# Polysketch attention, then an ELU feed-forward: group 0's division moved behind x, other rounding of the weights, z behind the keys' outer products

## The chip, the cores and the metric

The kernel runs on one core of a Trainium2 chip. The metric is the device time of one execution in microseconds (us). The weights and the sketches S1, S2 arrive as 64-bit floats, which the kernel reads as two 32-bit words each; q, k and v are float32.

## The reference

Four batches, four heads, 1088 positions, head size 32. Queries and keys are turned into features by two 8 x 32 sketches, and linear attention is formed with them; then comes a feed-forward layer with ELU.

```python
r = 8
def phi(x):                       # 64 features: outer product of two sketches
    a = np.einsum('rd,bhsd->bhsr', S1, x)
    b = np.einsum('rd,bhsd->bhsr', S2, x)
    return np.einsum('bhsi,bhsj->bhsij', a, b).reshape(*x.shape[:-1], r * r)
q_p, k_p = (phi(q), phi(k))
kv = np.einsum('bhsf,bhsd->bhfd', k_p, v)
z = np.sum(k_p, axis=2)
num = np.einsum('bhsf,bhfd->bhsd', q_p, kv)
den = np.einsum('bhsf,bhf->bhs', q_p, z)[..., None] + 1e-06
attn = num / den
...
h = x @ w_in                      # x: 4352 x 128, w_in: 128 x 2048
g = np.where(h > 0.0, h, np.exp(np.minimum(h, 0.0)) - 1.0)
out = g @ w_out                   # 2048 x 128
```

## The kernel before

**Groups and pairs.** The 4352 rows of x are cut into groups `g` of 512 columns; x of a group is held transposed (`xg[g]`, 128 features by 512 rows). The hidden layer of 2048 is cut into eight pairs `cp` of two 128-blocks `c`. `mm1(g, cp)` makes `h` in PSUM (four "h" banks, two for a step), `elu_a` is two ScalarE instructions (relu of -h, exp), `elu_d` one VectorE instruction that makes `gg`, and `mm2(g, cp)` sums the output. Every matmul is cut into column strips of 32 (`quarters`) and each shows as two records.

**Order.** The kernel gives every engine its instructions in the order in which the program names them (`manual_schedule`). Nothing is reordered: an instruction that waits holds all that is named after it on its engine. First come the setup and group 0 by hand, then group 1's queries mixed with the first steps, and then a loop over `steps`: (0,0), (0,1), (1,0), (1,1), (0,2), (1,2), (0,3), ... as (g, cp). Steps 0 and 1 are written by hand; the loop begins with step 2. In step n it does mm1, the work listed under `at(n)`, ELU of block 0, the work under `mid(n)`, ELU of block 1, the work under `late(n)`, and then mm2 (for group 1 `mm2_blocks`) of step n-2.

**Queries of group 0.** `q1_first` gives the two sketches of the queries (`abq`), `q1z_first` the sketch times z (`zqp`). `q2_den` multiplies and sums them to `den`, takes the reciprocal and multiplies one sketch by it (`an`); `q2_out` makes the outer products `qp`; `q4_early` turns them (`qtp`, copied to `qpT`); `q5_early` multiplies by the key sums `kvS` and copies to `xg[0]`. Group 1 goes the same way through `q1_second`, `q2(1, 2)`, `q4_early(1)`, `q5_early(1)`.

**Keys of batch 0.** `KF(0)` makes the sketches, `KO_pool` (POOL) the outer products of tiles 0 to 3, `KO_first` (VectorE) those of tiles 4, 5 and 6, 7 and 8, `KA(0)` the key sums in PSUM (`kv`), `KS_first` turns them into `kvS`. `Z` and `Z_out` give z's sketch in `SW`.

**Weights.** TensorE multiplies in float32, and the 64-bit weights are rounded in the kernel. They are loaded raw (`raw`, words lo and hi) on the SP queue, and a chunk `i` of `order` is rounded into `W`: chunks 0 and 1 are w_in of pairs 0 and 1, chunks 2 and 3 their w_out, 4 and 5 w_in and w_out of pair 2, chunks 6 to 10 all of pairs 3 to 7 (512 columns). The steps are `round_a` (VectorE), `round_b` (ScalarE), `round_s`, `round_m`, `round_d`, `round_e` (VectorE; for chunk 7 `round_e` on POOL). RA, RB, RC name them in groups.

Of the kernel before, what the change touches and what calls it, by code (L numbers as in the profile page):

```python
# [15 lines left out]
MUL, ADD, SUB, MAX = ALU.mult, ALU.add, ALU.subtract, ALU.max  # L16
AND, OR, SHL = ALU.bitwise_and, ALU.bitwise_or, ALU.logical_shift_left
EXP = mybir.ActivationFunctionType.Exp
RELU = mybir.ActivationFunctionType.Relu
AX = mybir.AxisListType.X  # L20
# [7 lines left out]
def kernel(  # L28
# [21 lines left out]
    nc = tc.nc  # L50
# [43 lines left out]
    nc.vector.memset(ebias[:], -float(896 << 23))  # L94
    tiny = const.tile([P, 1], F32, name="tiny")
    nc.gpsimd.memset(tiny[:], 2.0 ** -20)

# [17 lines left out]
    def round_s(raw, dst):  # L115
        d = dst.bitcast(U32)
        nc.vector.scalar_tensor_tensor(d, words(raw)[1], 0x80000000, d, op0=AND, op1=OR)

    def round_m(raw, dst):
        hi = words(raw)[1]  # L120
        nc.vector.tensor_scalar(hi, hi, 0x000FFFFF, 0x00100000, op0=AND, op1=OR)

    def round_c(raw, dst):
# [6 lines left out]

    def round_e(raw, dst, pool=False):
        mant = words(raw)[0].bitcast(F32)
        if pool:
            nc.gpsimd.tensor_mul(mant, mant, _ap(tiny[:], [[0, dst.shape[1]]]))  # L134
            nc.gpsimd.tensor_mul(dst, mant, dst)
        else:
            nc.vector.scalar_tensor_tensor(dst, mant, 2.0 ** -20, dst, op0=MUL, op1=MUL)

# [40 lines left out]
    def round_w(f, i, *a):  # L179
        if wide:  # L180
            cp, w_in, w_out = order[i]
            c = slice(0 if w_in else 2 * P, 4 * P if w_out else 2 * P)
            f(raw_w[cp][:, c], W[:, cp, c], *a)

    def RA(i):
        round_w(round_a, i)

    def RB(i):
        round_w(round_b, i)


    def RC_2():
        if wide:
            for f in (round_s, round_m, round_d):
                f(raw_2[:, :, :2 * P], W[:, :2, :2 * P])

    def RS(i):
        round_w(round_s, i)

    def RM(i):  # L200
        round_w(round_m, i)

    def RD(i):
        round_w(round_d, i)

    def RE(i):
        round_w(round_e, i)

    def RC(i, pool=False):
        round_w(round_c, i)  # L210
        round_w(round_d, i)
        round_w(round_e, i, pool)

# [207 lines left out]
    def z_tile(b, ps, i):  # L421
# [4 lines left out]
                         skip_group_check=True, tile_position=(0, c))  # L426

    def KA(b, halves=(0, 1)):
        if 0 in halves:
            kv_ps[b] = psum.tile([P, 512], F32, name="kv", **(dict(tag="aux") if b else dict(tag="o1", bufs=1)))  # L430
        kv = kv_ps[b]
        kp = {half: feats.pop((b, half)) for half in halves}
        for i in range(0 if 0 in halves else 5, KT if 1 in halves else 5):
            for h in range(H):
                nc.tensor.matmul(kv[32 * h:32 * h + 32, :R * R], vt[b][:, (h * KT + i) * D:(h * KT + i + 1) * D],  # L435
                                 kp[i // 5][:, i % 5, h].rearrange("p i j -> p (i j)"),
                                 start=(i == 0), stop=(i == KT - 1), skip_group_check=True, tile_position=(0, 32 * h))
            if b:
                z_tile(b, kv, i)

# [37 lines left out]

    def KS_first():
        kd = work.tile([P, 2, R * R], F32, name="kd", tag="kd", bufs=1)  # L480
        nc.scalar.copy(kd[:], _ap(kv_ps[0][:, :R * R], [[0, 2], [1, R * R]]))
        nc.tensor.transpose(kv_ps[0][:, 128:256], kd[:].rearrange("p w f -> p (w f)"), ident[:])
        nc.scalar.copy(kvS[:].rearrange("p h d -> p (h d)"), kv_ps[0][:, 128:256])
# [37 lines left out]
    def q1_second():  # L521
        p = psum.tile([P, 512], F32, name="abwp", tag="h", bufs=4)
        for i in range(4):
            for u in range(2):
                b, t = half_tile(1, 2 * i + u)
                nc.tensor.matmul(p[64 * u:64 * u + 64, i * 96:i * 96 + 96], qT[b][:, t, :],
                                 SW[:].rearrange("p h x r -> p (h x r)"), skip_group_check=True,
                                 tile_position=(0, 64 * u))
        abw[1] = work.tile([P, H * 4, 3 * R], F32, name="abw1", tag="abq1", bufs=1)
        nc.scalar.copy(abw[1][:].rearrange("p (h t) y -> p h t y", h=H),  # L530
                       p[:, :384].rearrange("p (t h y) -> p h t y", t=4, h=H))


# [47 lines left out]
    def q2_den(g, zq=None, between=None):  # L581
# [11 lines left out]
        nc.vector.tensor_reduce(den[:, :m], pw[:, :m], axis=AX, op=ADD)  # L593
        nc.vector.reciprocal(den[:, :m], den[:, :m])
        an = work.tile([P, 8 * H, R], F32, name="an", tag="an")
        nc.vector.tensor_mul(an[:, :m], x[:, :, R:2 * R], _ap(den[:, :m], [[1, m], [0, R]]))
        ans[g] = an

    def q2_out(g, parts=1, between=None):
        m = H * qn[g]  # L600
        x, an = abw.pop(g), ans.pop(g)
        qp[g] = work.tile([P, 4 * H, R, R], F32, name="qp", tag="qp", bufs=2)
        for i in range(parts):
            if i and between:
                between()
            h = slice(i * m // parts, (i + 1) * m // parts)
            a_ = an[:, h]
            b_ = x[:, h, :R]
            nc.vector.tensor_mul(qp[g][:, h], _ap(a_, list(a_.ap[1:]) + [[0, R]]),  # L609
                                 _ap(b_, [b_.ap[1], [0, R], b_.ap[2]]))  # L610

    def q4_early(g):

        qpT[g] = work.tile([P, H, 2, P], F32, name="qpT", tag="qpT", bufs=2)
        for hh in range(2):
            p = psum.tile([P, 512], F32, name="qtp", tag="aux")
            for h2 in range(2):
                for m in range(2):
                    o = (h2 * 2 + m) * P
                    r = (2 * hh + h2) * 4 + 2 * m  # L620
                    nc.tensor.transpose(p[:, o:o + P], qp[g][:, r:r + 2].rearrange("p t i j -> p (t i j)"), ident[:])  # L621
            nc.scalar.copy(qpT[g][:, 2 * hh:2 * hh + 2], p[:].rearrange("p (h m s) -> p h m s", h=2, m=2))

    def q5_early(g):
        xp = [psum.tile([P, 512], F32, name="xps", tag="aux") for _ in range(2)]
        for h in range(H):
            for w in range(2):
                nc.tensor.matmul(xp[w][D * h:D * h + D, :256], kvS[64 * w:64 * w + 64, h, :],  # L628
                                 qpT[g][64 * w:64 * w + 64, h].rearrange("p m s -> p (m s)"),
                                 skip_group_check=True, tile_position=(64 * w, D * h))  # L630
        xg[g] = work.tile([P, 512], F32, name="xg", tag="xg", bufs=3)
        to = xg[g][:].rearrange("p (m w s) -> p w m s", w=2, s=P)
        for w in range(2):
            nc.scalar.copy(to[:, w], xp[w][:, :256].rearrange("p (m s) -> p m s", s=P))  # L634

# [211 lines left out]
    def mm1_first():  # L847
        hs[0, 0] = [psum.tile([P, 512], F32, name="h", tag="h", bufs=4) for c in range(2)]
        for w in range(2):
            for c in range(2):  # L850
                cols = [x[:].rearrange("p (m w s) -> p w m s", w=2, s=P)[:, w] for x in (hs[0, 0][c], xg[0])]
# [23 lines left out]

    def mm2(g, cp, first, last):
        n = qn[g] * P
        if first:
            ops[g] = psum.tile([P, 512], F32, name="o", tag=f"o{g % 2}", bufs=1)
        gg = gs.pop((g, cp))  # L880
        for c in range(2):
            quarters(ops[g][:, :n], W[:, cp, (2 + c) * P:(3 + c) * P], gg[:, c, :n],
# [70 lines left out]
    KO_first(4, 5)  # L953
    KO_first(5, 7)
    Z(0, zps, zl)
    Z_out(0, zps)
    KO_first(7, KT)
    keep_warm(1, 96, 64)
    zq = q1z_first()
    q2_den(0, zq, lambda: RA(0))  # L960
    q2_out(0, 2, lambda: RA(1))
    KA(0)
    KS_first()
    keep_warm(1)
    RB(0)
    RB(1)
    q4_early(0)
    transp(qT, "q", 0, 8, NT)
    RC_2()
    RE(0)  # L970
    RE(1)
    q1_second()
    q5_early(0)
    keep_warm(1, 192, width[0])
    mm1_first()
    q2(1, 2, lambda: RA(2))
    RB(2)
    elu_a(0, 0, 0)
    elu_a(0, 0, 1, (0,))
    mm1(0, 1, (0,))  # L980
    q4_early(1)
    elu_d(0, 0, 0)
    mm1(0, 1, (1,))
    elu_a(0, 0, 1, (1,))
    RC(2)
    RA(3)
    elu_a(0, 1, 0, (0,))
    RB(3)
    q5_early(1)
    elu_d(0, 0, 1)  # L990
    mm2(0, 0, True, False)
    RA(4)
    for f in (RS, RM, RD):
        f(3)
    elu_a(0, 1, 0, (1,))
    elu_a(0, 1, 1)
    RB(4)
    elu_d(0, 1, 0)
    RE(3)
    elu_d(0, 1, 1)  # L1000


# [16 lines left out]

    at(2, RC, 4)  # L1020
    for n, i in ((4, 6), (5, 5), (6, 7), (8, 8), (10, 9), (12, 10)):
        at(n - 1, RA, i)
        late(n - 1, RB, i)
        at(n, RC, i, i == 7)

# [82 lines left out]
    for n in range(2, N):  # L1108
# [34 lines left out]
        elif g == 1:  # L1143
            mm2_blocks(cp)
        elif n > 2:
            mm2(g, cp, cp == 0, cp == NP - 1)
            if cp == NP - 1:
                fin1(g)
# [55 lines left out]
```

## Time and profile before

| | |
|---|---|
| median of 3 runs | 261.92 us (261.86 to 262.2) |
| span of the profiled execution (first to last instruction) | 260.6 us |
| the profiled execution's own time | not listed; the median lies 1.3 us above the span |
| granted TensorE clock | 0.998 of full |
| TensorE busy | 254.8 us (98%) |
| VectorE, ScalarE, POOL busy | 186.9, 183.4, 159.0 us |
| DMA moved | 15.61 MB |

The page names the engines PE (TensorE matmul), PEld (its weight loads), DVE (VectorE), ACT (ScalarE), POOL and SP. L256 is line 256 of the kernel before. The "chain that ended last" is followed back from the last instruction, at each step to what released it. A group of matmuls in a timeline starts where its first one starts and ends where the last one's modelled end lies, so successive groups overlap a little.

### The profile page before, as it was taken

How to read it: one execution, taken by the hardware profiler on the slowest of the kernel's cores; microseconds unless marked ns; L12 is line 12 of the kernel's file. 1: busy time of each engine (PE TensorE's matmuls, PEld its weight loads, DVE VectorE, ACT ScalarE, POOL GpSimd, SP SyncE). 2: the span in 40 equal slices, each digit the busy share in tenths (PEclk: the TensorE clock that was granted, in tenths of full speed). 3: DMA queues.
4: the chain of work that ended last, by engine and by line, in shares of the span. 5: the costliest groups of instructions: out<-in, count | busy, mean ns of one | idle time of the engine just before them, and what ended most of it. 6: DMA issues, size and time to landing. Idle time of an engine off the chain costs nothing.

```text
span 260.6 us, 9756 instructions
## 1 busy us (share of the span) xinstructions
PE 254.8 (98%) x4123; PEld 158.4 (61%) x4123; DVE 186.9 (72%) x352; ACT 183.4 (70%) x358; POOL 159.0 (61%) x202
## 2 busy tenths in 40 slices
PE   8899999999999999999999999999999999999994
PEld 6753333453346667666666666665666666668993
DVE  6799999999988967997477675744466746544651
ACT  2379968766667577776687777775877777777792
POOL 3520007002179996788678798888688888887310
PEclk9999999999999999999999999999999999999999
DMA  5998079012112210002100204220001110110021
GB/s 173 330 358 222 3 223 268 24 21 85 28 18 28 31 34 18 3 15 34 20 0 4 33 10 104 60 30 13 3 3 27 34 26 3 25 19 3 3 30 33
DMA packets 30379, 15.61 MB, mean 60 GB/s; under 512 B 22496, under 2 KB 28000, under 8 KB 30336
## 3 DMA queue, kind: packets, MB, share of 16 engines
q1 hardware_dynamic: 29904, 14.63, 23.0%
q8 instruction: 32, 0.52, 0.9%
q10 hardware_dynamic: 368, 0.30, 0.3%
q0 software_dynamic: 64, 0.07, 0.1%
q14 instruction: 11, 0.09, 0.1%
HBM read 11.31 MB, written 2.36 MB: 52 GB/s over the span
## 4 chain that ended last, share of the span: by engine, by line
PE 97%; DVE 1%; ACT 0%; issue 0%; DVEq 0%
PE h L256 45%; PE pb L790 17%; PE pa L790 13%; PE o L256 5%; PE pb L766 4%; PE ol L256 3%; PE idle L264 1%; PE kv L435 1%; PE abp L343 1%; PE h L681 1%; PE h L551 1%; PE qtp L621 1%; DVE qp L609 1%; PE h L693 1%; PE xps L628 0%; PE kfps L365 0%
## 5 line engine op out<-in xcount | busy, mean ns | idle before, releaser
L256 PE MATMUL h<-xg,W 128*32 128x512 f32 (+3 forms) x904 | 130.8, 539 | 0.4 <-ACT xg L634 0.4
L869 DVE SCALAR_TENSOR_TENSOR gg<-e,h 128x512 f32<-128x512 f32 x128 | 85.9, 681 | 52.6 <-ACT e L863 47.8
L861 ACT ACTIVATE e<-h 128x512 f32<-128x512 f32 x128 | 75.5, 590 | 46.2 <-PE h L256 46.0
L863 ACT ACTIVATE e<-e 128x512 f32<-128x512 f32 x128 | 80.9, 632 | 3.8
L751 POOL TENSOR_TENSOR tt<-gg 128x512 f32<-128x512 f32 x50 | 64.3, 1286 | 28.9 <-DVE gg L869 25.2
L256 PEld LDWEIGHTS h<-xg,W 128*32 128x32 f32 (+1 forms) x904 | 43.0, 122 | 43.0 <-issue 34.4
L754 POOL TENSOR_TENSOR tt<-gg,tt 128x256 f32<-128x256 f32 x50 | 36.9, 739 | 3.9
L753 POOL TENSOR_TENSOR tt<-tt,gg 128x256 f32<-128x256 f32 x50 | 36.7, 734 | 3.9
L790 PEld LDWEIGHTS pa<-gg,W 128*64 128x64 f32 (+1 forms) x496 | 23.7, 126 | 22.4 <-issue 22.2
L790 PE MATMUL pa<-gg,W 128*64 128x128 f32 (+1 forms) x496 | 30.6, 274 | 0.0
L790 PE MATMUL pb<-tt,SS 128*64 128x128 f32 (+1 forms) x480 | 29.6, 273 | 0.0
L790 PEld LDWEIGHTS pb<-tt,SS 128*64 128x64 f32 (+1 forms) x480 | 22.8, 126 | 0.0
L790 PE MATMUL pa<-tt,SS 128*32 128x128 f32 (+1 forms) x288 | 21.2, 273 | 0.0
L790 PE MATMUL pb<-gg,SS 128*64 128x128 f32 (+1 forms) x256 | 19.9, 273 | 0.0
L790 PE MATMUL pb<-tt,W 128*64 128x128 f32 (+1 forms) x256 | 19.9, 273 | 0.0
L134 POOL TENSOR_TENSOR raw<-raw,tiny 128x512 f32<-128x512 f32 x1 | 1.0, 1041 | 24.7 <-DVE raw L129 24.7
L256 PE MATMUL o<-gg,W 128*32 128x512 f32 x128 | 15.3, 595 | 0.0
L790 PEld LDWEIGHTS pa<-tt,SS 128*32 128x32 f32 (+1 forms) x288 | 13.7, 124 | 0.0
L790 PEld LDWEIGHTS pb<-gg,SS 128*64 128x64 f32 (+1 forms) x256 | 12.8, 125 | 0.0
L790 PEld LDWEIGHTS pb<-tt,W 128*64 128x64 f32 (+1 forms) x256 | 12.8, 125 | 0.0
L766 PE MATMUL pb<-gg,W 128*32 128x256 f32 x192 | 11.5, 380 | 0.0
L921 DVE SCALAR_TENSOR_TENSOR gg<-e,h 128x256 f32<-128x256 f32 x16 | 6.6, 418 | 6.4 <-PE h L256 3.2
(163 smaller groups left out, 269.3 us busy)
## 6 DMA issues: line engine op xcount, KB each, us to landing
raw<-in_moe_w_in_dram SPq DMA_DIRECT2D x8, 256.0 KB, 6.3
raw<-in_moe_w_out_dram SPq DMA_DIRECT2D x8, 256.0 KB, 6.5
out_dram<-ob SPq DMA_DIRECT2D x112, 16.0 KB, 1.5
hd_k<-in_k_dram SPq DMA_DIRECT2D x3, 544.0 KB, 7.5
hd_q<-in_q_dram SPq DMA_DIRECT2D x3, 544.0 KB, 8.5
v<-in_v_dram SPq DMA_DIRECT2D x4, 288.0 KB, 7.1
v<-in_v_dram SPq DMA_DIRECT2D x4, 256.0 KB, 8.4
raw<-qpF SPq DMA_DIRECT2D x16, 64.0 KB, 2.0
```

Of the source, the lines that this page charges most:

```text
L256: nc.tensor.matmul(dst[c:c + tile], lhs[:, c:c + tile], rhs, skip_group_check=True, tile_position=(0, c), **kw)
L264: nc.tensor.matmul(idle[c:c + tile, :cols], ones[:, :tile], ones[:, :cols], skip_group_check=True, tile_position=(0, c))
L343: nc.tensor.matmul(ps[i // 5][64 * u:64 * u + 64, 64 * (i % 5):64 * (i % 5) + 64], kT[b][:, u * KT + i, :], Sab[:].rearrange("p h y -> p ( ...
L751: nc.gpsimd.tensor_tensor(_ap(t[:, 0], [[4 * P, 2], [P, 2], [1, P]]), _ap(gs[g, cp][:, 0, P:], [[4 * P, 2]] + us), _ap(gs[g, cp][:, 0], [[ ...
L753: nc.gpsimd.tensor_tensor(t[:, 1], t[:, 2], b11, op=ADD)
L754: nc.gpsimd.tensor_tensor(t[:, 3], b21, t[:, 1], op=SUB)
L766: nc.tensor.matmul(acc[1][0][r:r + width[0], 256 * hi:256 * hi + 256], lhs[:, w:w + width[0]], gg[:, c, 256 * u:256 * u + 256], start=(cp ...
L790: nc.tensor.matmul(bank[r:r + width[0], P * col:P * col + P], lhs[:, w:w + width[0]], rhs[:, u], start=(first and i in ((0,) if g == 1 els ...
L861: nc.scalar.activation(e, hs[g, cp][c][:, :n], RELU, scale=-1.0)
L863: nc.scalar.activation(e, e, EXP, scale=-1.0)
L869: nc.vector.scalar_tensor_tensor(gs[g, cp][:, c, :n], es[g, cp][:, c, :n], -1.0, hs[g, cp][c][:, :n], op0=ADD, op1=MAX)
L921: nc.vector.scalar_tensor_tensor(gs["last", k // 2][:, k % 2, :2 * P], es["last", k // 2][:, k % 2, :2 * P], -1.0, hs["last", k][:, :2 * P ...
```

## The change

Five things are changed.

1. z: the third key product (`KO_first(7, KT)`) is named ahead of `Z` and `Z_out`; `KA_first` sums key tiles 4 to 8, then comes `q1z_first`, then tiles 0 to 3.
2. Group 0's queries are no longer divided ahead of the outer product. `q2_den` returns the reciprocals, `turn_den` spreads them over the rows of x with matmuls (two halves), ScalarE copies them to SBUF, and `q5_early_out` multiplies x by them as it leaves PSUM, on VectorE.
3. The rounding: `strip` (VectorE, or ScalarE for chunks 0 to 3), `floor` and `shift` (VectorE), `low` (ScalarE), `round_s` (VectorE), `whole` (POOL, an integer add).
4. The order from there to the loop: `mm1_first` goes block by block, `q1_second` comes behind it, mm1(0,1) is whole, q2 of group 1 stands behind both ELUs of step 0, and mm2(0,1) is done ahead of the loop.
5. In the loop chunks 5 to 10 are stripped, floored and shifted in `late(n)`, and signed and added in the middle of the step after.

```diff
     def round_s(raw, dst):
         d = dst.bitcast(U32)
-        nc.vector.scalar_tensor_tensor(d, words(raw)[1], 0x80000000, d, op0=AND, op1=OR)
+        nc.vector.scalar_tensor_tensor(d, words(raw)[1], 0x80000000, d, op0=AND, op1=XOR)
...
+    def strip(raw, dst, eng=nc.vector):
+        if eng is nc.vector:
+            nc.vector.tensor_scalar(dst.bitcast(U32), words(raw)[1], 0x7FFFFFFF, None, op0=AND)
+        else:
+            nc.scalar.activation(dst, words(raw)[1].bitcast(F32), ABS)
+    def floor(raw, dst):
+        nc.vector.tensor_scalar_max(dst, dst, 2.0 ** -15)
+    def shift(raw, dst):
+        nc.vector.tensor_scalar(dst.bitcast(U32), dst.bitcast(U32), 3, None, op0=SHL)
+    def low(raw, dst):
+        lo = words(raw)[0]
+        nc.scalar.activation(lo.bitcast(F32), lo, IDENTITY, scale=2.0 ** -51, bias=two[:dst.shape[0]])
+    def whole(raw, dst):
+        nc.gpsimd.tensor_tensor(dst.bitcast(U32), dst.bitcast(U32), words(raw)[0], op=ADD)
...
+    def R2(f, *a):
+        if wide:
+            f(raw_2[:, :, :2 * P], W[:, :2, :2 * P], *a)
+    def whole_0():
+        if wide:
+            for c in range(2):
+                whole(raw_2[:, 0, P * c:P * c + P], W[:, 0, P * c:P * c + P])
     def RA(i):
-        round_w(round_a, i)
+        for f in (strip, floor, shift):
+            R1(f, i)
     def RB(i):
-        round_w(round_b, i)
+        R1(low, i)
...
+    def RC(i):
+        R1(round_s, i)
+        R1(whole, i)
...
+    def KA_first(tiles, first, last):
+        if first:
+            kv_ps[0] = psum.tile([P, 512], F32, name="kv", tag="o1", bufs=1)
+        for i in tiles:
+            for h in range(H):
+                ...
...
+    def turn_den(den, w):
+        if w == 0:
+            feats["den"] = (psum.tile([P, 512], F32, name="denp", tag="h", bufs=4),
+                            work.tile([P, 2, 2 * P], F32, name="dent", tag="dent", bufs=1))
+        p, d = feats["den"]
+        for m in range(2):
+            o = (2 * w + m) * P
+            for h in range(H):
+                i = 4 * h + 2 * m + w
+                nc.tensor.matmul(p[D * h:D * h + D, o:o + P], _ap(den[:, i:i + 1], [[0, D]]), ident[:],
+                                 skip_group_check=True, tile_position=(0, D * h))
+        nc.scalar.copy(d[:, w], p[:, 2 * P * w:2 * P * w + 2 * P])
+        return d
...
+    def q5_early_out(g, xp, d=None):
...
+            x = xp[w][:, :256].rearrange("p (m s) -> p m s", s=P)
+            if d is None:
+                nc.scalar.copy(to[:, w], x)
+            else:
+                nc.vector.tensor_mul(to[:, w], x, d[:, w].rearrange("p (m s) -> p m s", s=P))
...
     def mm1_first():
-        for w in range(2):
-            for c in range(2):
+        for c in range(2):
+            for w in range(2):
...
     KO_first(5, 7)
+    KO_first(7, KT)
     Z(0, zps, zl)
     Z_out(0, zps)
-    KO_first(7, KT)
     keep_warm(1, 96, 64)
+    KA_first(range(4, KT), True, False)
     zq = q1z_first()
-    q2_den(0, zq, lambda: RA(0))
-    q2_out(0, 2, lambda: RA(1))
-    KA(0)
-    KS_first()
-    keep_warm(1)
-    RB(0)
-    RB(1)
-    q4_early(0)
+    KA_first(range(4), False, True)
+    R1(strip, 0, nc.scalar)
+    R1(low, 0)
+    q2_out(0, 2)
+    KS_first_a()
+    R1(strip, 1, nc.scalar)
+    q4_early(0, 0)
+    KS_first_b()
+    den = q2_den(0, zq)
+    q4_early(0, 1)
+    turn_den(den, 0)
+    R2(floor)
+    R2(shift)
+    R2(round_s)
+    whole_0()
+    x = q5_early(0)
+    den = turn_den(den, 1)
+    q5_early_out(0, x, den)
+    R1(low, 1)
+    R1(whole, 1)
+    keep_warm(1, 128, width[0])
+    mm1_first()
     transp(qT, "q", 0, 8, NT)
-    RC_2()
-    RE(0)
-    RE(1)
-    q1_second()
-    q5_early(0)
-    keep_warm(1, 192, width[0])
-    mm1_first()
-    q2(1, 2, lambda: RA(2))
-    RB(2)
+    R1(strip, 2, nc.scalar)
+    R1(low, 2)
+    R1(strip, 3, nc.scalar)
+    for f in (floor, shift, round_s, whole):
+        R1(f, 2)
+    abwp = q1_second()
     elu_a(0, 0, 0)
-    elu_a(0, 0, 1, (0,))
-    mm1(0, 1, (0,))
-    q4_early(1)
+    R1(low, 3)
     elu_d(0, 0, 0)
...
+    q1_second_out(abwp)
+    for f in (floor, shift, round_s, whole):
+        R1(f, 3)
+    mm1(0, 1)
+    elu(0, 0, 1)
+    q2(1, 2)
+    elu_a(0, 1, 0)
     mm2(0, 0, True, False)
+    elu_a(0, 1, 1)
+    q4_early(1, 0)
+    q4_early(1, 1)
+    elu_d(0, 1, 0)
+    elu_d(0, 1, 1)
+    mm2(0, 1, False, False, (0,))
+    x = q5_early(1)
+    q5_early_out(1, x)
+    mm2(0, 1, False, False, (1,))
     RA(4)
...
     RB(4)
+    RC(4)
...
-    at(2, RC, 4)
-    for n, i in ((4, 6), (5, 5), (6, 7), (8, 8), (10, 9), (12, 10)):
-        at(n - 1, RA, i)
-        late(n - 1, RB, i)
-        at(n, RC, i, i == 7)
+    for n, i in ((3, 6), (4, 5), (5, 7), (7, 8), (9, 9), (10, 10)):
+        late(n, RA, i)
+        late(n, RB, i)
+        mid(n + 1, RC, i)
...
-        elif n > 2:
-            mm2(g, cp, cp == 0, cp == NP - 1)
+        elif n > 3:
+            mm2(g, cp, False, cp == NP - 1)
```

## The prediction

> **What bounds the kernel now.** I read the page first, for the busy shares and the chain that ended last, to see which engine sets the end.
>
> ```profile
> span 260.6 us, 9756 instructions
> ...
> PE 254.8 (98%) x4123; PEld 158.4 (61%) x4123; DVE 186.9 (72%) x352; ACT 183.4 (70%) x358; POOL 159.0 (61%) x202
> ...
> PE 97%; DVE 1%; ACT 0%; issue 0%; DVEq 0%
> ```
>
> TensorE is the chain. Second, the chain in order of time, to see where it leaves TensorE and what TensorE does next to the edited stretch.
>
> ```profile
> 11.69 0.69 DVE qp L609
> 12.50 0.70 DVE qp L609
> 13.34 0.63 PE qtp L621 x4
> 13.96 0.85 PE abwp L526 x16
> 14.81 0.70 PE xps L628 x16
> 15.52 0.64 ACT xg L634 x2
> 16.25 2.79 PE h L256 x40
> ...
> 23.51 3.43 PE h L256 x32
> 26.94 1.72 PE o L256 x16
> ...
> 35.67 1.72 PE h L256 x16
> ```
>
> Columns are start, length, engine and tile. Up to 16.25 us the chain hops between engines; from 16.25 it stays on TensorE, and from 23.51 each block of 16 matmuls follows the last at its bare 1.72 us. The waits view names for TensorE 1.9 us in all, every one before 23.51. So nothing that frees VectorE after 23.51 can gain; the change can only move the moment at which TensorE reaches 23.51's work, or open new gaps behind it. The run of blocks from there is: mm1(1,0) and mm1(1,1) (23.51), mm2(0,1) (26.94), mm1(0,2), blocks(1,0), mm1(1,2), blocks(1,1), mm1(0,3) (35.67).
>
> Third, the timeline of the other engines, for durations and for slack.
>
> ```profile
> 29.39 0.69 DVE L869 SCALAR_TENSOR_TENSOR gg<-e,h 128x512 f32<-128x512 f32 x1 [0.45 <-ACT e L863]
> 30.00 0.24 DVE L444 STREAM_TRANSPOSE kvt<-kv 128x64 f32<-128x64 f32 x1
> 32.90 1.34 DVE L280 STREAM_TRANSPOSE kT<-hd_k 128x1088 f32<-128x1088 f32 x1
> 41.54 1.31 POOL L135 TENSOR_TENSOR W<-raw,W 128x512 f32<-128x512 f32 x1
> 42.19 0.96 DVE L102 TENSOR_SCALAR W<-raw 128x512 uint32<-128x512 uint32 x1
> ```
>
> The first is the last ELU result of step 3; between the second and third VectorE rounds chunk 6 (the weights of pair 3), which therefore stand at 32.78, long before 35.67. The last two bear on a collision: L102 takes 0.44 alone (27.81) and 0.96 beside the POOL operation.
>
> **The parts, one by one.** Two lengths matter per operation: until the next may start on its engine, and until the result is seen. On ScalarE a 256-column copy takes 0.37 and the next starts 0.09 before its end; L107 (with a bias operand) 0.51; an ELU pair L861+L863 1.26, or 1.17 to the next. On VectorE L102 takes 0.29 (256) or 0.44 (512), a two-tensor operation 0.42 or 0.69. Engine to engine costs 0.05 to 0.25.
>
> *z behind the outer products.* VectorE does the third key product (0.69, no longer behind L465) right after the second, at 8.92 instead of 9.43, then SW. TensorE does key tiles 4 to 8 (done 10.07, after that product at 9.6), zq (0.62), tiles 0 to 3 (32 of 72 matmuls of 1.21 us: 0.54), end 11.23 instead of 11.36. Gain 0.13.
>
> *Division moved.* q2_out no longer waits for the reciprocal: qp is done at 11.0 instead of 13.2. The denominators (0.29+0.33+0.25) follow behind it, unhurried. ScalarE becomes the path. From the sums' end at 11.23: kd from 11.33, strip of chunk 1 (0.31), first qpT copy 11.91 to 12.50, kvS, second qpT copy 12.65 to 13.24. TensorE: xps from 13.34 (0.60), second turn of the denominators. This turn is new: 16 matmuls of 128 columns in four strips; bounded below by bare streaming, 16/16 of 1.72 us x 128/512 = 0.43, above by the 0.70 of 16 xps matmuls; I take 0.45, since xps has twice the columns. So 14.39, dent copy 14.49 to 14.86, product out of PSUM (0.42, the row of the 256-column kp) 14.89 to 15.31. The first half of x is there at 14.46.
>
> *Rounding of chunks 0 and 1.* strip is an Abs: no row, so an immediate-only activation of 256, 0.40 (between 0.28, half a 512 copy, and 0.51). VectorE: floor, shift 0.46 each (a dependent 512), sign 0.65, from 11.94 to 13.51. The raw words land in time: issued at 3.96 and 5.23, landing 5.5 and about 5.8 later (the DMA view), so at 9.5 and 11.0; strip 0 runs from 9.55, strip 1 from 11.51. POOL adds two 128-column pieces: L289 has 0.40 for 128 columns; 13.56 to 14.40. Hidden behind xps; without that cover each 0.1 later would move the start 0.1. First matmul of h at 14.62 instead of 16.25, its second half, which needs the second half of x, at 15.36.
>
> Whether Abs and Identity cost a reload of ScalarE's table isn't shown: the one load took 1.28 us (L155), and Copy, Relu and Exp then alternate with no other. I take no load; two (there and back) bound it above at 2.6 us. [...]
>
> *From h to mm1(1,0).* ScalarE has strip 2, low 2 and strip 3 queued ahead of the first ELU, which starts at 16.23 (h was ready at 16.1): to 17.49. Then low 3 (0.42) and the abw1 copy (0.39, q1_second now lies behind mm1_first on TensorE), second ELU 18.21 to 19.47, gg 19.50 to 20.12. Only then VectorE does q2 of group 1, which before came ahead of the first gg at 16.35: 0.29+0.33+0.29+0.32+0.60+0.60, to 22.55; then both gg of (0,1), seen 23.29 and 23.86. TensorE has finished mm2(0,0) at 21.20 and waits to 22.09 for qp, does both transposes, waits for gg, and starts the first half of mm2(0,1) at 23.29: 0.86 (+0.1 restart) + 0.60 xps + 0.86 = 25.71, where mm1(1,0) starts. Before, the same work (mm2(0,1) included) ends at 23.51+1.72 = 25.23. The same arithmetic on the order of before gives 16.10 and 23.12 for 16.25 and 23.51, 0.39 too early; like for like the difference is 25.71-(23.12+1.72) = **0.87 lost**. So the 1.6 us won at the first matmul are gone.
>
> *Steps 3 to 6.* mm2(0,1) no longer lies behind mm1(1,1), so TensorE reaches mm1(0,3) one block sooner after the ELU of step 3: 35.67-29.39-1.72 = 4.56 after that gg starts. ScalarE's ELU pairs run back to back there before and after, so gg doesn't move with it. But chunk 6 is now rounded later: strip, floor and shift after that gg, then KT_out's transpose, the kT transpose at the head of step 4, gg(0,2,0), and only in the middle of step 4 the sign, then POOL. VectorE: 0.62+0.44+0.46+0.46+0.24+1.30+0.62+0.65 = 4.79; POOL's integer add of 512: 1.31 (the row above, same shape and strides; the integer form has no row: 0.7 to 2.6), hops 0.1: 6.20. mm1(0,3) waits 6.20-4.56 = **1.64**, with the restart 1.74. Queued behind it on TensorE is everything. The later release of the raw buffer also holds the SP queue some 5 us (pair 7's weights and the next k, v, q were issued from 32.81); pair 7 is wanted after 50 us and those later, so nothing.
>
> Later rounding is cheaper on VectorE by 0.9 per 512 (L129 and L137 gone, one pass more), worth nothing under TensorE's chain.
>
> Sum: 0.87+1.74 = 2.6 us, on the median of 261.92: **264.5**. The span is 260.6, with 1.3 around it; the profiled execution's own time isn't listed, so I carry the same 1.3.
>
> [...] L102 beside POOL took 0.96 and L117 1.72 beside L322 (0.69 alone), each ending about 0.5 after POOL did. [...]
>
> **Rivals.**
> - *The lead is kept (faster).* q2 of group 1 and chunk 6 come in time, and TensorE streams from the second half of x: its work to mm1(1,0) is 1.72+0.85+1.72+1.72+1.02+0.86+0.60+0.86 = 9.35, so 15.36-0.43+9.35 = 24.28, 0.95 ahead of 25.23, **261.0**; with x's first half followed at once it would be 260.3. For: VectorE is relieved, and the waits are all short. Against: q2 would have to be over before 21.2 and ends at 22.5; ScalarE's queue decides.
> - *Only the first loss.* The POOL add at 0.7 and quicker dependent VectorE passes leave under 0.6 at mm1(0,3): 262.8 to 263.3. The point is chunk 6 standing 4.56 after the gg.
> [...]
> - *No change.* ScalarE's steps 0.1 shorter each at eleven places on the path give back 0.9, and chunk 6 is nearly on time: 262.0.
>
> **How the numbers follow.** Forecast (both waits) 0.45, first loss only 0.17, more waits 0.12, lead kept 0.20, no change 0.06. A difference within 0.2% (0.5 us) is about what can't be told from none. Slower 0.45+0.17+0.12 = 0.74, same 0.06, faster 0.20. The range leaves out half the lead-kept case below and most of the widest waits above: 261.0 to 266.0; the forecast's own range is 263.4 to 265.4 (the POOL add at 0.7 to 1.9).
>
> **What would show it.** Right: first h matmul near 14.6 with a short gap before 15.4; a gap of some 0.9 before group 1's qtp transposes, released by VectorE's qp; mm1(1,0) near 26; blocks of 1.72 after it up to mm1(0,3), which waits 1.7 for W, released by POOL's add, with the kT transpose ahead of the sign step. Wrong: no PE wait after mm1(1,0), or mm1(1,0) before 25.2; a second table load; POOL's add far from 1.3.

## The result and the profile after

The changed kernel takes **268.12 us** (median of 6 runs, 267.79 to 269.93) against 261.89 for the kernel before (6 runs on the same chip, 261.83 to 262.2): a ratio of **1.0254** [1.023, 1.0278], slower by 6.2 us. The forecast of 264.5 us had the sign, but 268.12 lies 2.1 us above the top of its range.

The profiled execution took 269.79 us with a span of 268.0; in all six runs the time is 1.8 to 1.9 us above the span. First the page of the changed kernel, the busy shares, the granted clock and the chain's shares:

```profile
span 268.0 us, 9841 instructions
...
PE 257.4 (96%) x4153; PEld 157.9 (59%) x4153; DVE 180.6 (67%) x339; ACT 185.1 (69%) x362; POOL 166.4 (62%) x212
...
PEclk9999979999999999999999999999999999999999
...
PE 89%; ACT 3%; DMA 2%; issue 1%; DVE 1%; SPq 1%; DVEq 0%
```

TensorE's share of the chain fell from 97% to 89%: the chain now leaves TensorE for other engines. VectorE does 6.3 us less work than before and nothing comes of it. The single 7 in the clock row is one slice of 6.7 us around 36 us. Where the chain left TensorE is in the waits view, for PE (us in total, times, longest):

```profile
PE pb L811 <- DVE kvt L462: 2.6, 1, 2.6
PE denp L657 <- issue: 1.6, 1, 1.6
PE qtp L645 <- DVE qp L634: 0.9, 1, 0.9
```

The first two have no counterpart in the waits view of before. Nor has the third, which is group 1's (a wait of `qtp` for `qp` of 0.2 there is group 0's); it alone was in the prediction. The chain in order of time shows where each one lies (start, length, what):

```profile
13.08 0.86 PE xps L666 x16
13.94 0.34 PE denp L657 x2
14.27 1.55 issue
15.83 0.53 PE denp L657 x11
...
23.49 0.70 DVE qp L634
24.19 0.04 issue
24.24 1.26 PE qtp L645 x8
...
28.18 0.91 PE h L263 x8
...
35.70 0.26 DVE kvt L462
35.96 0.04 issue
36.00 3.38 PE pb L811 x32
39.38 1.72 PE h L263 x16
41.09 1.73 PE pb L811 x32
42.82 1.72 PE h L263 x16
```

The second turn of the denominators starts at 13.94, the very time in the prediction, though in part by luck: `xps` ahead of it started 0.26 sooner and took 0.26 longer than forecast. Then TensorE stands for 1.55 us in the middle of these 16 matmuls, waiting for nothing that the profile shows. mm1(1,0) starts at 28.18; the same work ended at 25.23 before: **+2.95**. (Executions differ ahead of h: the kernels of experiments 1 and 2 that are the same up to there reach these points 0.43 and 0.32 sooner, which makes it 2.84.) blocks(1,0) (`pb`) starts at 36.00 instead of 30.37, that is +5.63, of which 2.65 is its wait for KT_out's transpose (`kvt`). It then takes 3.38 instead of its usual 1.73: **+1.65**. mm1(0,3), at 35.67 before, starts at 42.82, so 7.15 of the 7.4 us by which the span grew lie ahead of it. (The three parts add up to 7.25; blocks(1,0) took 1.85 and not 1.73 before.)

VectorE's timeline around the second wait (start, length, line, operation, tiles; in brackets the idle time ahead and what ended it):

```profile
33.84 0.69 DVE L914 SCALAR_TENSOR_TENSOR gg<-e,h 128x512 f32<-128x512 f32 x1 [0.46 <-ACT e L908]
34.45 0.42 DVE L127 TENSOR_SCALAR W<-raw 128x512 uint32<-128x512 uint32 x1
34.90 0.43 DVE L132 TENSOR_SCALAR W<-W 128x512 f32<-128x512 f32 x1
35.36 0.43 DVE L135 TENSOR_SCALAR W<-W 128x512 uint32<-128x512 uint32 x1
35.70 0.24 DVE L462 STREAM_TRANSPOSE kvt<-kv 128x64 f32<-128x64 f32 x1
```

KT_out(0) reads the key sums `kv` in PSUM. That tile has the tag "o1" with one buffer, and `mm2_blocks(0)` takes the same tag for `pb`. Before, KT_out's transpose followed the last gg of step 3 at once (30.00, done 30.24), and blocks(1,0) began at 30.37. Now strip, floor and shift of chunk 6 lie between them.

The long block is a matter of the clock. The stretches of 1 us (busy time and count by engine, then the granted clock in the third column from the end):

```profile
35.00:36.00 1.00, 0.00 (x0) 0.00 (x1) 0.96 (x4) 1.00 (x2) 0.00 (x0) 0.78 0.00 0
36.00:37.00 1.00, 1.00 (x12) 0.54 (x16) 1.00 (x1) 0.97 (x3) 0.00 (x0) 0.50 0.00 0
37.00:38.00 1.00, 1.00 (x16) 0.45 (x12) 1.00 (x3) 0.17 (x1) 0.00 (x0) 0.50 0.00 0
38.00:39.00 1.00, 1.00 (x16) 0.41 (x12) 1.00 (x3) 0.00 (x0) 0.56 (x1) 0.51 0.00 0
39.00:40.00 1.00, 1.00 (x16) 0.35 (x12) 0.97 (x2) 0.00 (x0) 0.74 (x1) 1.00 0.00 0
```

The clock was at half for some 3.4 us from about 35.55, that is 2.2 us after TensorE had run dry at 33.34. Two of the six executions have a lower mean clock (269.79 and 269.93, at 0.993 and 0.994); the other four, at 0.999 to 1.0, took 267.79 to 268.15. Where the clock fell is known of the profiled one alone. There the wait cost its 2.65 and the clock another 1.65; in four of the six the second part is missing.

### The profile page after: what moved, and what is told of

Its sections match the earlier page's. It is cut to its first block, busy times and chain, and to the rows that moved or that the text cites. A ratio compares the mean times of both kernels' runs of the same rounds, so it can differ in the third digit from the quotient of the medians.

```text
span 268.0 us, 9841 instructions
## 1 busy us (share of the span) xinstructions
PE 257.4 (96%) x4153; PEld 157.9 (59%) x4153; DVE 180.6 (67%) x339; ACT 185.1 (69%) x362; POOL 166.4 (62%) x212
## 4 chain that ended last, share of the span: by engine, by line
PE 89%; ACT 3%; DMA 2%; issue 1%; DVE 1%; SPq 1%; DVEq 0%
PE h L263 41%; PE pb L835 16%; PE pa L835 13%; PE o L263 5%; PE pb L811 4%; PE ol L263 3%; DMA v<-in_v_dram 2%; PE kv L454 1%; ACT e L908 1%; ACT e L906 1%; PE qtp L645 1%; PE h L726 1%; PE h L573 1%; PE denp L657 1%; PE xps L666 1%
## 5 line engine op out<-in xcount | busy, mean ns | idle before, releaser
L142 POOL TENSOR_TENSOR W<-W,raw 128x256 uint32<-128x256 uint32 (+2 forms) x12 | 11.1, 930 | 39.8 <-DVE W L119 27.7
L811 PE MATMUL pb<-gg,W 128*32 128x256 f32 x192 | 12.9, 416 | 2.6 <-DVE kvt L462 2.6
L811 PEld LDWEIGHTS pb<-gg,W 128*32 128x32 f32 x192 | 6.4, 120 | 10.0 <-issue 3.8
```

The lines of the kernel that those rows point to most:

```text
L142: nc.gpsimd.tensor_tensor(dst.bitcast(U32), dst.bitcast(U32), words(raw)[0], op=ADD)
L811: nc.tensor.matmul(acc[1][0][r:r + width[0], 256 * hi:256 * hi + 256], lhs[:, w:w + width[0]], gg[:, c, 256 * u:256 * u + 256], start=(cp ...
```

## Experiments

**1. KT_out ahead of chunk 6, then chunk 6 a step sooner.** The theory: the bank that KT_out frees is what blocks(1,0) waits for; and behind that wait the forecast wait of mm1(0,3) for chunk 6 is hidden.

```diff
-    late(3, KT_out, 0)
+    late(2, KT_out, 0)          # named ahead of the rounding loop
     for n, i in ((3, 6), (4, 5), (5, 7), (7, 8), (9, 9), (10, 10)):
```

> The changed kernel with KT_out(0), VectorE's transpose of the key sums, one step earlier (end of step 2 instead of step 3, ahead of chunk 6's rounding). Theory (bank): in the changed kernel blocks(1,0) needs the PSUM bank of kv, and that transpose, its last reader, stands behind three rounding passes, so TensorE stands 2.65 us and in some executions then runs at half clock for 1.65. Without it blocks(1,0) follows mm1(0,2) at once, and the next late thing is chunk 6, whose POOL add ends some 5.7 us after the gg of step 3's second block, 1.1 us after mm1(0,3) wants it: net gain 1.5 us against an unthrottled execution, 266.6 us, clock 1.00 in all. Rival (the rounding of chunk 6 alone holds TensorE, the bank is free anyway): no change, 268.1.

Measured: 266.99 us (266.59 to 268.35), 1.0209 [1.018, 1.0239]. A full clock in all executions was expected; the longest of the four (268.35) had 0.992, without the wait for the bank. The profile, clock 1.00, has no wait for `kvt`. The waits view of PE, and the line of PE's timeline at the new place:

```profile
PE denp L657 <- issue: 1.4, 1, 1.4
PE h L263 <- POOL W L142: 1.2, 1, 1.2
PE qtp L645 <- DVE qp L634: 0.9, 1, 0.9
```

```profile
39.28 1.92 PE L263 MATMUL h<-xg,W 128*32 128x512 f32 x16 [1.18 <-POOL W L142]
```

The wait for the bank is gone and the wait of mm1(0,3) for chunk 6 stands where the prediction put it, at 1.18 us instead of 1.74. In the changed kernel it was hidden: without the 2.65 and the 1.65, mm1(0,3) would have been reached at 38.52, 1.22 ahead of chunk 6 (39.74).

In the second kernel chunk 6 is stripped in step 2 as well:

```diff
-    for n, i in ((3, 6), (4, 5), (5, 7), (7, 8), (9, 9), (10, 10)):
+    for n, i in ((2, 6), (4, 5), (5, 7), (7, 8), (9, 9), (10, 10)):
```

> As e1, and chunk 6 is stripped, floored and shifted at the end of step 2 and finished in the middle of step 3, one step earlier. Theory (two late things in a row, bank first, chunk 6 second): neither holds TensorE, blocks of 1.72 from mm1(1,0) on; 265.4 us, 1.2 less than e1. Rival (only the bank): equal to e1 within 0.3. Rival (VectorE's added work ahead of the gg of step 3 makes a new wait at mm1(1,2)): above e1.

Measured: 265.48 us (265.34 to 265.98), 1.0138 [1.0123, 1.0153]. From mm1(1,0) on TensorE runs without a wait. So two edits of order give back 2.6 us of the 6.2. What is left lies ahead of mm1(1,0), which starts at 28.66 in this profile against 25.23: 3.4 of the 3.5 us between the spans (264.1 and 260.6). The profile is of the longest of the four executions, 265.98, and part of its 3.4 is a wait of TensorE for a load:

```profile
PE kv L440 <- DMA v<-in_v_dram: 1.0, 1, 1.0
```

The first key sums, now ahead of `q1z_first`, wait here for v's load. The changed kernel's profile has 0.4 of this wait, the profile of 266.59 none.

**2. KT_out late in the kernel before.** The converse: the old kernel, with nothing changed but the place of this one transpose.

```diff
-    late(3, KT_out, 0)
+    at(4, KT_out, 0)            # behind the kT transpose
```

> The kernel before with one thing changed: KT_out(0) (VectorE's transpose of the key sums, done at 30.24 us) stands behind the kT transpose of step 4, at about 34.3. Theory (bank): blocks(1,0) stands from 30.4 to about 34.5 on that transpose, +4.1 us, and the granted clock falls to half for some us after it in part or all executions, up to +1.7: 266.0 to 267.7. Rival (nothing reads that bank so soon): no change, 261.9.

Measured: 267.53 us (265.98 to 267.74), 1.0198 [1.0174, 1.0223]. PE's timeline, in the execution of 265.98:

```profile
33.90 1.93 PE L766 MATMUL pb<-gg,W 128*32 128x256 f32 x32 [3.86 <-DVE kvt L444]
```

One VectorE operation of 0.24 us, put 3.6 us later, costs 4.0 us at a full clock. The other three executions, at a mean clock of 0.994, took 267.51 to 267.74, another 1.6 us. In this execution TensorE waited 3.86 us and the clock stayed full, so the length of the wait alone doesn't decide whether it drops.

**3. What is the gap of 1.55 us?** In the changed kernel 221 weight loads and 221 matmuls start ahead of the gap, so it ends at record 443. (The expectations below call it 449, and the first of them 523; the trace has 443.) The theory, an estimate that no view names: there TensorE's queue runs out of instructions and the next ones are still on their way. The page has a queue for instructions with 32 packets and 0.52 MB, 16 KB each, and the first of these begins 2.4 to 2.6 us ahead of record 443 in each kernel of this table; where a kernel of this table has the gap, it ends at record 443:

```
kernel                       first packet   record 443 starts   between
before                          12.81            15.34            2.53
after                           13.43            15.82            2.39
KT_out ahead of chunk 6         12.98            15.39            2.41
36 more records (below)         15.56            18.12            2.56
loads held (below)              13.07            15.51            2.44
```

In the kernel before record 443 opens the warm-up matmuls ahead of h. Its weight loads there, and below them the same group in the first kernel of experiment 4, where it begins with record 407:

```profile
15.34 0.16 PEld L264 LDWEIGHTS idle<-const-float32-1.0 128*32 128x32 f32 x8 [0.41 <-issue]
15.24 0.16 PEld L271 LDWEIGHTS idle<-const-float32-1.0 128*32 128x32 f32 x8 [0.41 <-issue]
```

The pause is the same at both counts, so it is the ordinary one ahead of this group: the trace of before doesn't show the gap. TensorE came to record 443 there 2.53 us after the packet, about when it goes on in the others.

The first test shifts the count: 18 more matmul records and as many weight loads in the first warm-up.

```diff
-    keep_warm(3)
+    keep_warm(12, 64)
```

> The changed kernel, with the first three 256-column warm-up matmuls cut into twelve of 64 columns: the same columns, but 36 more TensorE records ahead of everything. In the changed kernel TensorE stands 1.55 us in the midst of turn_den's second half, after some 523 records, for nothing that the profile names. Theory (the next 16 KB of TensorE's instructions, one of 32 packets of the instruction queue, arrive too late): the gap moves to an earlier place in the program by 36 records, into xps, and stays as long or grows, since its end is set by the packet and not by the place; time 268 to 269. Rival (something of turn_den's second half itself, its one-column weights or the copy of its first half): the gap stays in turn_den's second half with the same length, 268.1.

Measured: 271.89 us (271.45 to 272.74), 1.0383 [1.0363, 1.0404]. PE's timeline:

```profile
18.12 0.67 PE L666 MATMUL xps<-qpT,kvS 64*32 64x256 f32 x16 [2.34 <-issue]
```

The gap left the turn of the denominators and stands ahead of `xps`, the group of 16 matmuls that comes before it, at record 443 again: it goes with the count and not with the operation. The time, 268 to 269 expected, says less, since the warm-up itself grew to 6.20 us from 3.65 and pushed everything later. The wait for `kvt` (2.6) was unmoved.

The second test asks whether the packet is late behind the loads of weights and inputs. The loads that fill the DMA engines at 13 to 16 us (share 1.06 to 1.11 in the changed kernel) are held until POOL's first addition.

```diff
-    for b in range(1, B): ...   # loads of pairs 3 to 7 and of batches 1 to 3
+    raw_w[3] = work.tile(...)   # the same loop, behind whole_0
+    nc.gpsimd.memset(raw_w[3][:, :1, :], 0)
```

> The changed kernel, with the loads of pairs 3 to 7 and of batches 1 to 3 held until POOL has done its two first adds (a one-column memset of a raw buffer stands behind them), so that the DMA engines, 100% busy from 3 to 20 us, are free from about 12 to 15 us. Theory (the instruction packet waits behind the loads): the gap of 1.55 us in turn_den's second half shrinks below 0.5 and mm1(1,0) starts 1 to 2 us earlier: 266.2 to 267 with the wait at blocks(1,0) still there. Rival (not a fetch): the gap stays, 268.1. Second rival: the held loads come late for chunk 6 or the keys of batch 1 and TensorE waits there instead.

Measured: 269.84 us (268.35 to 270.0), 1.0288 [1.026, 1.0316]. The stretch with the gap (last two columns: DMA share and GB/s), and the waits view of PE:

```profile
13.00:14.00 1.00, 1.00 (x18) 0.31 (x16) 0.59 (x2) 0.34 (x2) 0.37 (x1) 1.00 0.15 41
14.00:15.00 1.00, 0.09 (x1) 0.00 (x0) 0.33 (x1) 0.00 (x0) 0.53 (x3) 1.00 0.00 0
```

```profile
PE pb L805 <- DVE kvt L456: 2.6, 1, 2.6
PE denp L651 <- issue: 1.4, 1, 1.4
```

The DMA engines are idle and the gap is still 1.4: this half of the theory falls. The extra 1.7 us over the changed kernel goes with the clock: three of the four executions, at 0.993 to 0.994, took 269.77 to 270.0, and the fourth, at 1.0, 268.35.

The third test, on the kernel of 265.48, puts both turns of the denominators ahead of `xps`, so that other work stands at record 443.

```diff
     turn_den(den, 0)
+    den = turn_den(den, 1)
...
     x = q5_early(0)
-    den = turn_den(den, 1)
```

> e2 with both halves of turn_den ahead of xps on TensorE. Theory (the gap sits at a count of TensorE records, 449, and ends 2.4 to 2.6 us after the first 16 KB instruction packet begins): the gap of 1.2 to 1.5 us now stands right ahead of xps, named issue, and since xps then starts near 15.4 the second half of x comes out when it did: 265.4 us, within 0.3 of e2. Rival (the gap belongs to turn_den's second half behind xps): no gap ahead of xps, h complete 1.5 us earlier, 263.9.

Measured: 265.66 us (265.2 to 266.63), 1.0134 [1.0118, 1.0149]. PE's timeline:

```profile
15.68 1.10 PE L666 MATMUL xps<-qpT,kvS 64*32 64x256 f32 x14 [1.47 <-issue]
```

The gap moved into `xps`; the time is the same within 0.2. Reordering two groups at the gap doesn't avoid it: everything behind record 443 waits for it alike. The 1.10 for 14 matmuls is the clock: this profile is of the longest execution (266.63), and its clock fell to half as the gap ended (columns as above):

```profile
14.00:15.00 1.00, 0.22 (x1) 0.00 (x0) 0.00 (x0) 1.00 (x4) 0.58 (x2) 1.00 1.06 359
15.00:16.00 1.00, 0.32 (x7) 0.22 (x14) 0.00 (x0) 0.57 (x2) 0.34 (x1) 0.81 1.11 375
16.00:17.00 1.00, 1.00 (x22) 0.20 (x8) 0.07 (x1) 0.00 (x0) 0.00 (x0) 0.50 1.03 359
```

So the gap, like the wait for the bank, can cost a stretch at half clock on top. That TensorE waits for instructions there is inferred from the count and the packet, in three arrangements; the profile names only "issue". Two kernels below fit it from the other side: where TensorE came to record 443 only 3.1 and 3.4 us after the packet began (`v2_chunk0_first`, `e6_divide_before`), it shows no gap of this kind. What starts the packet when it starts isn't settled. If it is this packet that TensorE waits for, the wait isn't hidden behind other work, at 1.2 to 2.3 us in these kernels.

**4. Division against order.** What is left of the loss is split by undoing one at a time. First the division goes back ahead of the outer product, in the kernel of 265.48:

```diff
     R1(low, 0)
+    q2_den(0, zq)
     q2_out(0, 2)
...
-    den = q2_den(0, zq)
...
-    turn_den(den, 0)
...
-    den = turn_den(den, 1)
-    q5_early_out(0, x, den)
+    q5_early_out(0, x)
```

> e2 with the division of group 0 put back ahead of the outer product (no turn_den; ScalarE copies x out of PSUM), all else as e2. Theory (turn_den costs more than the earlier qp gains, because its second half is caught by the gap at TensorE's record 449 and x's second half waits for the copy behind it): the first block of h is complete some 1.2 us earlier than in e2, 264.2 us. Rival (the late division is what won time, and everything else lost it): slower than e2 by the 1 to 1.3 us that the reciprocal and its product take, 266.6.

Measured: 264.64 and 264.93 us, 1.0106 [1.0088, 1.0125] (two further executions took 446 and 1495 us and are left out). mm1(1,0) starts at 27.35, and no gap of the kind of experiment 3 shows.

Then the order goes back: the rounding of the changed kernel, with the division, z and everything up to the loop named as in the kernel before, and KT_out and chunks 6, 5 and 7 a step earlier.

```diff
-    KO_first(7, KT)
     Z(0, zps, zl)
     Z_out(0, zps)
+    KO_first(7, KT)
...
+    q1_second_out(q1_second())
+    q5_early_out(0, q5_early(0))
...
     mm1_first()
+    q2(1, 2)
...
-    for n, i in ((3, 6), (4, 5), (5, 7), (7, 8), (9, 9), (10, 10)):
+    late(2, KT_out, 0)
+    for n, i in ((2, 6), (3, 5), (4, 7), (7, 8), (9, 9), (10, 10)):
```

> The rounding of the changed kernel in the order of before: division ahead of the outer product, q1_second ahead of xps, group 1's q2 ahead of the first gg, mm2(0,1) in step 3; KT_out and chunk 6 as in e2. Theory (the loss is the new order and the turned division, not the rounding): W of pairs 0 and 1 and x stand 0.5 to 0.7 earlier than 16.25, since VectorE does two passes less ahead of qp and one long pass less ahead of h, and no wait opens behind: 261.2 to 261.5 us, just faster than before. [...]

Measured: **261.67 us** (11 runs, 261.44 to 261.93) against 262.01: 0.9987 [0.9978, 0.9996], 0.3 us faster than the kernel before. In this order the rounding by integer steps costs nothing: h starts at 15.51, against 16.25 in the profile of before and 15.92 in that of experiment 2, whose code is the same as before up to there. How much of the 0.3 is the rounding's, and not that of the earlier KT_out and chunks, wasn't told apart.

And this kernel with the late division:

```diff
-    q2_den(0, zq)
     q2_out(0, 2)
+    den = q2_den(0, zq)
...
+    turn_den(den, 0)
...
-    q5_early_out(0, q5_early(0))
+    x = q5_early(0)
+    den = turn_den(den, 1)
+    q5_early_out(0, x, den)
```

> v1 with the division of group 0 moved behind x (turn_den's first half ahead of q1_second, its second behind xps, product out of PSUM), so that division and order are told apart: v1 is early division in the order of before, e6 early division in the new order, e2 late division in the new order. Theory (the late division loses in either order, since xps then starts at TensorE's record 449, near 15.0, and the second half of x waits for the turn, its copy and the product, to 17.0 instead of 15.6): 1.1 us over v1, 262.8. Rival (the late division loses only in the new order, where q1_second isn't there to fill): within 0.3 of v1, 261.7.

Measured: 263.31 us (262.98 to 263.5), 1.0041 [1.0026, 1.0056], 1.6 more. The expectation, 262.8, had the gap ahead of `xps`; it stands at the last matmul of `abwp` (0.64), one record sooner, 2.6 us after its packet (12.59), and the second half of h at 17.59:

```profile
15.22 0.24 PE L546 MATMUL abwp<-SW,qT 128*64 128x96 f32 x1 [0.64 <-issue]
15.40 0.66 PE L666 MATMUL xps<-qpT,kvS 64*32 64x256 f32 x16
15.99 0.64 PE L657 MATMUL denp<-ident,den 128*32 128x128 f32 x16
```

The four together, with KT_out and chunk 6 early in all (the columns also differ by the place of z, and by chunks 5 and 7, a step earlier in the order of before):

```
                        order of before    new order
division early               261.67          264.8
division late                263.31          265.5
```

The order costs 2.2 to 3.1 us, with z's place, worth 0.5 in experiment 5, in it. With the division early in both, mm1(1,0) starts at 27.35 in the new order against 22.76 + 1.72 = 24.48 for the same work in the old one, 2.87 later: 0.39 is the start of h (15.90 against 15.51), 0.85 are q1_second's matmuls, now behind h, 0.88 is the wait for group 1's qp; the other 0.75 wasn't taken apart. The late division costs 0.7 to 1.6 (the 0.7 rests on two executions of one kernel): it saves the reciprocal's stretch on VectorE ahead of the outer product, and puts two turns, a copy and a product onto the same path.

**5. z, and chunk 0 first.** The new place of z in the kernel of 261.67:

```diff
+    KO_first(7, KT)
     Z(0, zps, zl)
     Z_out(0, zps)
-    KO_first(7, KT)
+    KA_first(range(4, KT), True, False)
     zq = q1z_first()
+    KA_first(range(4), False, True)
```

> v1 with z behind the third key product and the key sums of tiles 0 to 3 behind zq, as in the changed kernel. My prediction took this part as a gain of 0.13 on the key sums. Theory (with the division early the denominators lead, and zq comes about 0.5 later, so qp, xps and h come 0.3 to 0.5 later): 262.0 to 262.2. Rival (the key sums lead, the gain counts): 261.5.

Measured: 262.21 us (11 runs, 262.16 to 263.02), 1.0011 [1.0002, 1.002]: 0.5 worse than without it. The third key product (0.69) now lies ahead of the queries on VectorE, and TensorE's timeline has

```profile
12.57 1.32 PE L642 MATMUL qtp<-ident,qp 128*128 128x128 f32 x8 [0.47 <-DVE qp L631]
```

Last, chunk 0 is rounded ahead of chunk 1 and the warm-up ahead of h left out, in the kernel of 261.67:

```diff
-    R2(floor)
-    R2(shift)
-    R2(round_s)
+    for f in (floor, shift, round_s):
+        R1(f, 0)
     whole_0()
+    for f in (floor, shift, round_s):
+        R1(f, 1)
...
-    keep_warm(1, 192, width[0])
```

> v1 with chunk 0 rounded ahead of chunk 1 instead of both at once, and without the warm-up matmuls ahead of h. Theory (h in v1 waits for POOL's first add, 15.42, as much as for x, 15.33): h starts 0.1 to 0.15 earlier, 261.5 us, hardly to be told from v1. Rival (TensorE's record 449 then lies in h itself and its gap, ending near 15.0, shows): no change or up to 0.3 slower.

Measured: 261.64 us (261.53 to 261.93), 0.9986 [0.9977, 0.9995], the same as 261.67. h starts at 15.50, against 15.51. POOL's first add now ends at 14.9, but its second, which the profile names as what h waits for (0.61), ends at 15.39, and the first half of x is there at 15.35, no sooner than in the kernel of 261.67 (15.34). The rival, a gap in h itself, doesn't show: record 443 is h's first weight load, at 15.47.

## Why the prediction was wrong, point by point

- **What bounds the kernel: right.** TensorE's chain decides, and 6.3 us less VectorE work gained nothing.
- **z behind the outer products, a gain of 0.13: not found.** The key sums end at 11.36, as before. Their first part waited for v's load until 9.42 (0.41), which the prediction didn't look at, and that wait was 1.00 in another execution (experiment 1). In the order of before the new place costs 0.5 (experiment 5); in the new order its price alone wasn't measured.
- **Group 0 to the second half of x, 15.36: mis-sized, 17.41.** The hops were nearly right: xps at 13.08 (13.34 forecast) for 0.86 (0.60), second turn at 13.94 (13.94), from its end to h 0.91 (0.97). The wrong term is "I take 0.45" for the second turn: it lasted from 13.94 to 16.50. Of these 2.56 us 1.55 are the gap at record 443 and 1.01 the matmuls in two pieces. In one piece the turn keeps within the bounds of 0.43 to 0.70: 0.57 for the first turn, 0.62 for the second where the gap lay elsewhere (36 more records). Bounds taken from rows of matmuls couldn't hold the gap, and the trace of before doesn't show it (experiment 3).
- **From h to mm1(1,0): right.** Forecast 10.35 from the second half of x, or 10.59 with the 0.24 by which the same arithmetic fell short on this stretch of before; measured 28.18 - 17.41 = 10.77. The wait for group 1's qp was forecast at 0.9 and is 0.88. The like-for-like loss of 0.87 became 2.95 by the 2.05 by which the second half of x came late.
- **Steps 3 to 6: the step that failed worst.** The prediction named KT_out's transpose as 0.24 of VectorE in a queue that it was itself moving behind three passes, and didn't ask who waits for what it reads. The answer, blocks(1,0) through the one buffer of "o1", had a margin of 0.13 in the trace of before (30.24 against 30.37). Its price: 2.65, and 1.65 more where the clock fell. "Blocks of 1.72 after it up to mm1(0,3)" was wrong by this.
- **The wait of mm1(0,3), 1.74: real, but hidden.** It shows as 1.18 once the bank is free (experiment 1). Chunk 6 stood 39.74 - 33.84 = 5.90 after the gg, where 6.20 was forecast; POOL's integer add took 1.30 for the 1.31 taken. The 0.1 for TensorE's restart in the 1.74 was the author's estimate, and no run shows it: behind the wait of 3.86 the next block started 1.76 after this one, against 1.73 without a wait (timelines of experiments 2 and 1). In the changed kernel it costs nothing, so the 264.5 contained a term that wasn't paid and lacked two that were.
- **Table of ScalarE: right; VectorE beside POOL: no cost.** The trace has one table load (1.28 us), none around the Abs of 0.43 to 0.45. A 256-column strip beside POOL's add took 1.07 instead of 0.29 and ended 0.16 after it (the rows that the prediction read as about 0.5 give 0.30 and 0.55), and no wait of TensorE came of that.
- **Rivals.** "More waits", at 0.12, had the direction, but the waits that came were those for `kvt` (2.65) and in the gap (1.55). "Only the first loss" and "no change" fall with the time. "The lead is kept" falls too: there was no lead, since h's second half started at 17.41 against 16.25 for all of h before.

## What to carry to other kernels

When work is put into an in-order queue, ask of every small instruction behind it which buffer it sets free and who takes that buffer next: a transpose of 0.24 us, moved by 3.6 us, cost 4.0 us of TensorE. When a stretch is made shorter, ask what else paced it: in the trace of before TensorE came to record 443 2.53 us after the first packet of the instruction queue, and work that was moved ahead of that moment ran into a gap that this trace doesn't show. And a wait that shows first hides the next one: free the first and look again before the sum is called complete.

## What the runs showed of the hardware

- TensorE stood for 0.6 to 2.3 us at its 443rd load or matmul record (in one kernel a record sooner), 2.3 to 2.6 us after the first 16 KB packet on the instruction queue began, with the DMA engines full (share 1.06 at 14 to 15 us) or idle (0.00). Where it came there 3.1 and 3.4 us after the packet, no such gap stood.
- In profiles the clock fell to half 2.2 us into a wait of 2.65, and at the end of a gap of 1.47, the first time for 3.4 us, the second, by the mean clock of 0.994, for about as long; in a wait of 3.86 it stayed full. The mean clock was down in 2 of 6 executions of the changed kernel, in 3 of 4 where the loads were held, and in 3 of 4 with the wait of 3.86. What decides whether it falls isn't shown by these runs.
- Narrow warm-up matmuls were dear: the first group took 6.20 us for 26 matmul records, most of 64 columns, where 8 records of 256 and 224 columns had taken 3.65. A quarter of the columns came to 0.24 us each against 0.46, about half and not a quarter. The 36 matmuls of `abp` behind them took 2.79 as well, against 2.11.
